# The sequence transform's four groups in one block, and E columns ahead of the tables' copies

## The chip, the cores and the metric

The kernel runs on one core of one Trainium2 chip. The metric is the device time of one execution in microseconds. A core has five engines with queues of their own: TensorE (PE, with weight loads shown as PEld), VectorE (DVE), ScalarE (ACT), GpSimd (POOL) and SyncE (SP), which here issues nearly all DMA transfers. Each engine works through its queue in order and waits for the others by semaphores. In this kernel the order is fixed by hand: the program text's order is the order in every queue.

## The reference

```python
X = np.fft.fft(x, axis=1)          # x: 8 batches, 3008 positions, 256 features
X = np.fft.fft(X, axis=2)
x = X.real.reshape(8 * 3008, 256)
gate = 1.0 / (1.0 + np.exp(-(x @ w_gate)))      # w_gate, w_val: 256 x 1536
val = x @ w_val
out = gate * val @ w_out                        # w_out: 1536 x 256
```

All is float32. The kernel uses the symmetries of the real transform: for a batch it computes three tables over positions k, pk (cosine part), qk (sine part) and ek (the contribution of feature 128, called E here), each of 1505 columns, and gets the hidden values of positions k and S - k from sums and differences of products of these.

## The kernel before

The main loop has 576 steps. A batch has 72 steps, in 6 chunks of 256 positions (the last has 225), and a chunk has 12 steps, one for each 128 hidden features. A step multiplies with pk and qk (front), forms the hidden product of the step before (gate), and adds to the output of two pairs of steps before (back):

```python
def front(p, fh):
    ...
    for g in range(2):
        mm(pa[:, g], G1[:, g, fs], pk[:, ks], g == 0, True)
    for g in range(2):
        mm(pb[:, g], G2[:, g, fs], qk[:, ks], g == 0, True)
    for g in range(2):                          # VectorE
        nc.vector.scalar_tensor_tensor(out=ae[:, g], in0=ek[:, ks], scalar=ge[:, g, f : f + 1],
                                       in1=pa[:, g], op0=ALU.mult, op1=ALU.add)
    nc.vector.tensor_tensor(z[:, :, 0], ae, pb, op=ALU.add)
    nc.vector.tensor_tensor(z[:, :, 1, ::-1], ae, pb, op=ALU.subtract)

def gate(p, fh, z):
    nc.vector.tensor_tensor(h[:, fh], z[:, 0], z[:, 1], op=ALU.mult)
    # ... then one or three sums sf of h on GpSimd

def back(p, part):
    for m in ORDER[part]:                       # 3 or 4 matmuls of h and sf into PO
        mm(PO[t][:, j, 0:n], wf[:, i, m - 1], move[m], ...)
```

A matmul of float32 stands in the trace as two records. The tiles pa, pb, ev, od and pe share four PSUM banks, which are given out in turn (psx, bufs=4). A bank is free when what reads it has read it.

Beside these steps, one batch ahead, the next batch's pk and qk are made. Its input x is first copied within DRAM into a mirrored form (mirror_x: xr), loaded (load_x: x4, one buffer), folded on GpSimd in 24 operations (fold_ops), and then transformed in four groups, one for each parity of k (blk) and each of cosine and sine (what). A group is 12 matmul pairs, the two of a pair on the two halves of the rows:

```python
    def both():
        for r in range(2 - blk):
            for q in range(N3 if blk == 0 else NQ):
                for par, sum_ in enumerate((ev, od)):
                    ...
                    mm(sum_[:, ks], w(wq)[rows], ST[0][rows, int(sn), q, c0 : c0 + n][:, ks], ...)

    def then():
        a = evp.tile([P, NE], F32, name="a", tag="a")[:, 0:n]
        nc.scalar.copy(a, ev)
        return lambda: places(d, blk, sn, a, od)       # two sums on VectorE into pk or qk

def whole(b, blk, what):
    _, then, both = seq_group(b, blk, what)
    both()
    return then()
```

The E tables of batches 1 to 7 are made together, once: e_load(b) loads feature 128 of a batch (single values of 4 bytes), e_fold adds on GpSimd, e_sums multiplies on TensorE and writes the result to DRAM, from where a batch's ek is loaded later. The tables of the transform (stab) are copied within DRAM into mirrored form too (mirror_tables: tr), and loaded again in that form (table_again), which all groups of batches 1 to 7 read.

Work of this kind is put at the end of numbered steps:

```python
def at(i, *fs):                # do fs at the end of step i
    side.setdefault(i, []).extend(fs)

def split(i, f, *args):        # f at step i, what it returns at step i + 1
    at(i, lambda: at(i + 1, f(*args)))
```

Of the kernel before, what the change touches and what calls it, by code (L numbers as in the profile page):

```python
# [51 lines left out]
def kernel(  # L52
# [57 lines left out]
    def load_x(b):  # L110
        X[b] = xp.tile([P, 4, NQ, D], F32, name="x4", tag="x4")
        for h in range(0, 4, 2):
            if b:
                nc.sync.dma_start(out=X[b][:, h : h + 2], in_=XR[b][:, h : h + 2])
            else:
                nc.sync.dma_start(out=X[b][0:NP, h : h + 2], in_=xf[b, :, h : h + 2])

    def mirrored(dst, src, full):


        copy = nc.sync.dma_start
        h, n = dst.shape[1], dst.shape[3] - full
        ops = [lambda: copy(out=dst[HP - 2 : HP, :, NQ - 1, full:],  # L123
                            in_=zero[:, :, 0:n].to_broadcast([2, h, n]))]

        def rows(par):
            copy(out=dst[par * HP : (par + 1) * HP, :, 0:N3], in_=src[0:HP, :, par:NQ:2])  # L127

        def mirror(par, q):
            t = M // 2 - 2 * q - par  # L130
            lo, p0, n = par * HP, t // NQ, HP - 2 * ((par, q) == (0, N3 - 1))
            copy(out=dst[lo : lo + n, :, N3 + q, full:].rearrange("p h d -> h p d"),  # L132
                 in_=src[p0 - n + 1 : p0 + 1, :, t % NQ, full:].rearrange("p h d -> h p d")[:, ::-1])
        for par in range(2):
            ops.append(lambda par=par: rows(par))
            ops += [lambda par=par, q=q: mirror(par, q) for q in range(N3)]
        return ops
# [3 lines left out]
    def mirror_x(b):  # L141
        XR[b] = dram.tile([P, 4, NQ, D], F32, name=f"xr{b}")
        return mirrored(XR[b], xf[b], 0)
# [17 lines left out]
    def mirror_tables():  # L161
        return mirrored(tr, stab, NE)
# [213 lines left out]
# [5 lines that stand above are left out]
    def seq_start(b):  # L381
        PQE[b] = (pqp.tile([P, NK], F32, name="pk", tag="pk"),
                  pqp.tile([P, NK], F32, name="qk", tag="qk"),
                  pqp.tile([P, NK], F32, name="ek", tag="ek"))
        if b:
            nc.sync.dma_start(out=PQE[b][2], in_=ed[b - 1 : b, :].to_broadcast([P, NK]))

    def seq_group(b, blk, what, other=None):
        return half(lambda q: W[b, blk][what][:, q, :], PQE[b][what], blk, what == 1, other)


    def e_load(b):
        nc.sync.dma_start(out=x8[:, b - 1], in_=xf[b, :, :, :, HD : HD + 1])  # L393
# [216 lines left out]
    def at(i, *fs):  # L610
        side.setdefault(i, []).extend(fs)

    def split(i, f, *args):

        at(i, lambda: at(i + 1, f(*args)))
# [11 lines left out]
        at(2 * c + (-3, -2, 1)[w], lambda j=j: weight_use(j))  # L627


    i0 = 2 * NPR  # L630
    quiet = lambda lo: (i for i in range(lo, 2 * len(pairs)) if not 3 <= i % i0 <= 7)
    calm = lambda lo: (i for i in range(lo, 2 * len(pairs)) if 3 <= i % i0 <= 7)
# [2 lines left out]
    at(i0 + 2, lambda: load_x(1))  # L635
    for b in range(1, B):
        at(i0 + 2 + b, lambda b=b: e_load(b))
    for i, f in zip(range(i0 + 3, 2 * i0), mirror_tables()):
        at(i, f)
    at(2 * i0 + 3, e_fold)  # L640
    split(2 * i0 + 5, e_sums)
    at(2 * i0 + 8, table_again)

    for b in range(B - 1):
        s0 = b * per
        if b:
            at(s0 - 5, lambda b=b: load_x(b + 1))

        def folds(f0=s0 - 1 if b else i0 + 8, b=b):
            for i, f in zip(quiet(f0), fold_ops(b + 1, 2)):  # L650
                at(i, f)
        at(s0 - 2 if b else i0 + 7, folds)
        groups = [s0 + i0 * k + 3 for k in (2, 3, 4, 5)] if b else [
            i0 * k + d for k in (4, 5) for d in (3, 6)]
        at(groups[0] - 2, lambda b=b: seq_start(b + 1))
        for j, g in enumerate(groups):
            split(g, whole, b + 1, 1 - j // 2, j % 2)
        if b < B - 2:
            for i, f in zip(calm(s0 + 2 * i0 + 9), mirror_x(b + 2)):
                at(i, f)  # L660

    fresh = None
# [72 lines left out]
```

## Time and profile before

| | |
|---|---|
| time, median of 3 | 2010.83 us (2010.72 to 2019.48) |
| span of the profiled execution | 2008.0 us |
| instructions | 28130 |
| granted TensorE clock, mean | 0.995 |
| DMA | 100.32 MB, mean 50 GB/s |

In the profile's rows an engine, an operation and its tiles are named as out<-in, and L100 is the helper that all matmuls go through, so matmuls are told apart by tiles. Busy time of an engine is not the same as use: a matmul's start-to-start distance shows what it costs in a stream, and is shorter than its duration, as matmuls are pipelined. SPq is SyncE's queue of DMA issues.

### The profile page before, as it was taken

The page shows a single profiled execution, that of the slowest core. Times are in us where ns is not written, and L with a number is a line of the kernel's source. Part 1 is how long each engine was busy: PE and PEld are TensorE (multiplying, and loading weights), DVE is VectorE, ACT ScalarE, POOL GpSimd, SP SyncE. Part 2 cuts the span into 40 slices and gives each one's busy share as a digit, 9 for nine tenths or more (in the row PEclk, how much of TensorE's full clock was granted, in tenths as well). Part 3 has the DMA queues.
Part 4 walks back from the last instruction along what each step waited for, and adds up shares of the span by engine and source line. Part 5 has one row for each costly group of instructions (what it writes and reads, how often), then busy time and mean ns, then how long its engine had stood idle before and what let it go on. Part 6 is the DMA issues. An engine that isn't in the chain of part 4 may idle for free.

```text
span 2008.0 us, 28130 instructions
## 1 busy us (share of the span) xinstructions
PE 1975.4 (98%) x9504; PEld 1738.0 (87%) x9504; DVE 1767.0 (88%) x3221; ACT 498.3 (25%) x876; POOL 1332.2 (66%) x1704
## 2 busy tenths in 40 slices
PE   6998999999999999999999999999999999999998
PEld 4887889888998889888898888988889888998888
DVE  7997988988899888998889888898889997898887
ACT  3422222222222222222222222222222222222221
POOL 3676867775578655777567765677657775555655
PEclk9998999999999999999999999999999999999999
DMA  7355202111200112001120011201211010000001
GB/s 270 93 142 139 81 11 75 23 51 46 74 20 27 43 43 83 12 27 43 48 79 10 27 48 48 74 10 32 69 41 55 15 32 11 11 16 16 11 16 26
DMA packets 160814, 100.32 MB, mean 50 GB/s; under 512 B 128419, under 2 KB 151715, under 8 KB 157994
## 3 DMA queue, kind: packets, MB, share of 16 engines
q1 hardware_dynamic: 158850, 98.00, 16.9%
q8 instruction: 76, 1.25, 0.3%
q10 hardware_dynamic: 1822, 0.54, 0.1%
q14 instruction: 66, 0.54, 0.1%
HBM read 73.74 MB, written 50.17 MB: 62 GB/s over the span
## 4 chain that ended last, share of the span: by engine, by line
PE 92%; DMA 3%; SPq 3%; DVE 1%; issue 0%; ACT 0%; POOL 0%; ACTq 0%; DVEq 0%; POOLq 0%
PE po L100 41%; PE pa L100 23%; PE pb L100 23%; PE ev L100 4%; SPq L132 1%; DMA ge<-G 1%; DMA st<-in_stab_dram 1%; SPq L127 1%; DMA xr<-in_xf_dram 1%; SPq L123 0%; PE ps L100 0%; DMA x<-in_xf_dram 0%; PE od L100 0%; SPq L393 0%; DMA raw<-in_moe_w_gate_dram 0%
## 5 line engine op out<-in xcount | busy, mean ns | idle before, releaser
L672 ACT ACTIVATE z<-z 128x512 f32<-128x512 f32 (+1 forms) x576 | 358.5, 622 | 1308.2 <-DVE z L451 1308.2
L447 DVE SCALAR_TENSOR_TENSOR ae<-ek,ge,pa 128x256 f32<-128x256 f32 (+1 forms) x1152 | 488.4, 464 | 159.4 <-PE pa L100 155.1
L100 PE MATMUL pa<-pk,G 128*128 128x256 f32 (+1 forms) x2304 | 585.4, 377 | 0.0
L100 PE MATMUL pb<-qk,G 128*128 128x256 f32 (+1 forms) x2304 | 582.1, 375 | 2.5 <-DVE ae L447 2.5
L100 PE MATMUL po<-sf,wf 128*128 128x256 f32 (+1 forms) x2304 | 534.7, 375 | 0.0
L466 POOL TENSOR_TENSOR sf<-h 128x256 f32<-128x256 f32 (+1 forms) x288 | 206.9, 718 | 443.4 <-DVE h L462 443.4
L100 PEld LDWEIGHTS pa<-pk,G 128*128 128x128 f32 x2304 | 436.8, 191 | 59.6 <-issue 11.9
L100 PEld LDWEIGHTS pb<-qk,G 128*128 128x128 f32 x2304 | 438.3, 190 | 52.7 <-DVE ae L447 4.1
L100 PEld LDWEIGHTS po<-sf,wf 128*128 128x128 f32 x2304 | 438.7, 191 | 48.8 <-POOL sf L468 0.3
L462 DVE TENSOR_TENSOR h<-z 128x512 f32<-128x512 f32 (+1 forms) x576 | 471.4, 818 | 0.0
L450 DVE TENSOR_TENSOR z<-ae,pb 128x512 f32<-128x512 f32 (+1 forms) x576 | 390.0, 677 | 61.3 <-DVE ae L447 1.8
L100 PE MATMUL po<-h,wf 128*128 128x256 f32 (+1 forms) x1728 | 412.7, 375 | 0.0
L451 DVE TENSOR_TENSOR z<-ae,pb 128x512 f32<-128x512 f32 (+1 forms) x576 | 386.4, 671 | 0.0
L100 PEld LDWEIGHTS po<-h,wf 128*128 128x128 f32 x1728 | 329.0, 190 | 36.4
L464 POOL TENSOR_TENSOR sf<-h 128x256 f32<-128x256 f32 (+1 forms) x288 | 206.4, 717 | 128.8 <-DVE h L462 118.5
L468 POOL TENSOR_TENSOR sf<-h,sf 128x256 f32<-128x256 f32 (+1 forms) x288 | 213.5, 741 | 22.6
L467 POOL TENSOR_TENSOR sf<-sf,h 128x256 f32<-128x256 f32 (+1 forms) x288 | 207.2, 719 | 22.6
L100 PE MATMUL ev<-st,x 63*128 63x376 f32 (+4 forms) x372 | 103.2, 420 | 6.7 <-DVE x L290 5.4
L100 PE MATMUL od<-st,x 63*128 63x376 f32 (+4 forms) x372 | 102.5, 418 | 0.0
L100 PEld LDWEIGHTS ev<-st,x 63*128 63x128 f32 (+1 forms) x372 | 65.1, 188 | 38.6 <-DVE x L290 5.8
L549 ACT COPY c<-po 128x512 f32<-128x512 f32 (+1 forms) x141 | 76.3, 579 | 47.7 <-PE po L100 47.1
L509 DVE STREAM_TRANSPOSE os<-c 128x256 f32<-128x256 f32 x192 | 83.8, 436 | 0.2
(91 smaller groups left out, 808.9 us busy)
## 6 DMA issues: line engine op xcount, KB each, us to landing
x<-xr SPq DMA_DIRECT2D x14, 1536.0 KB
out_dram<-os SPq DMA_DIRECT2D x288, 64.0 KB
xr<-in_xf_dram SPq DMA_DIRECT2D x14, 768.0 KB
xr<-in_xf_dram SPq DMA_DIRECT2D x35, 256.0 KB
ek<-ed SPq DMA_DIRECT2D x7, 752.5 KB
out_dram<-os SPq DMA_DIRECT2D x92, 56.0 KB
x<-in_xf_dram SPq DMA_DIRECT2D x2, 1512.0 KB
tr<-in_stab_dram SPq DMA_DIRECT2D x2, 1129.5 KB
```

Source lines behind the costliest of these rows:

```text
L100: nc.tensor.matmul(o, l, r, start=start, stop=stop, skip_group_check=True)
L447: nc.vector.scalar_tensor_tensor(out=ae[:, g], in0=ek[:, ks], scalar=ge[:, g, f : f + 1], in1=pa[:, g], op0=ALU.mult, op1=ALU.add)
L450: nc.vector.tensor_tensor(z[:, :, 0], ae, pb, op=ALU.add)
L451: nc.vector.tensor_tensor(z[:, :, 1, ::-1], ae, pb, op=ALU.subtract)
L462: nc.vector.tensor_tensor(h[:, fh], z[:, 0], z[:, 1], op=ALU.mult)
L464: tt(s[:, 2], h[:, 0, 0], h[:, 0, 1], op=ALU.subtract)
L466: tt(s[:, 0], h[:, 0, 1], h[:, 1, 1], op=ALU.add)
L467: tt(s[:, 1], s[:, 0], h[:, 0, 0], op=ALU.subtract)
L468: tt(s[:, 3], h[:, 1, 0], s[:, 1], op=ALU.subtract)
L509: nc.vector.transpose(os_[:, s, 0:nb, h, :], t[:, slot, 0 : nb * TB])
L549: nc.scalar.copy(t[:, 2 * j : 2 * j + 2, 0:n], PO[j][:, :, 0:n])
L672: nc.scalar.activation(z[:, 0], z[:, 0], AF.Sigmoid)
```

## The change

Four things move; no operation is added, removed or altered.

- The four groups of a batch stand one after another at the end of one step (3 i0 + 3 steps into the batch before; for batch 1 at step 5 i0 + 3), where they stood in four steps, in four chunks (for batch 1 in two). The sums on VectorE that follow a group come right after it, not a step later. The purpose is to change between the two kinds of matmul once in a batch.
- The copies of the tables start after the E columns are loaded (step 2 i0 - 2, before at i0 + 3, interleaved with them); the fold of E comes 9 steps later, its sums 10 steps later, and the reload of the tables 9 steps later.
- The load of x for a batch follows the block directly (before: 5 steps ahead of the next batch).
- The folds start 16 steps ahead of the batch in whose time they ran (for batch 2, 4 steps; for batch 1 as before), and the mirrored copies of x come earlier in the batch.

In the diff i0 is 12 steps, one chunk, per is 72, and quiet and calm are the steps of a chunk outside and inside positions 3 to 7.

```diff
-    for i, f in zip(range(i0 + 3, 2 * i0), mirror_tables()):
-        at(i, f)
-    at(2 * i0 + 3, e_fold)
-    split(2 * i0 + 5, e_sums)
-    at(2 * i0 + 8, table_again)
+    for i, f in enumerate(mirror_tables()):
+        at(2 * i0 - 2 + i, f)
+    at(3 * i0, e_fold)
+    split(3 * i0 + 3, e_sums)
+    at(3 * i0 + 5, table_again)
 
     for b in range(B - 1):
         s0 = b * per
-        if b:
-            at(s0 - 5, lambda b=b: load_x(b + 1))
-
-        def folds(f0=s0 - 1 if b else i0 + 8, b=b):
+        g0 = s0 + 3 * i0 + 3 if b else 5 * i0 + 3
+
+        def folds(f0, b=b):
             for i, f in zip(quiet(f0), fold_ops(b + 1, 2)):
                 at(i, f)
-        at(s0 - 2 if b else i0 + 7, folds)
-        groups = [s0 + i0 * k + 3 for k in (2, 3, 4, 5)] if b else [
-            i0 * k + d for k in (4, 5) for d in (3, 6)]
-        at(groups[0] - 2, lambda b=b: seq_start(b + 1))
-        for j, g in enumerate(groups):
-            split(g, whole, b + 1, 1 - j // 2, j % 2)
+        f0 = s0 - 4 * i0 // 3 if b > 1 else 5 * i0 + 8 if b else i0 + 8
+        at(f0 - 1, lambda f0=f0, folds=folds: folds(f0))
+        at(g0 - 2, lambda b=b: seq_start(b + 1))
+        for blk in (1, 0):
+            at(g0, *[lambda b=b, blk=blk, what=what: whole(b + 1, blk, what)() for what in range(2)])
         if b < B - 2:
-            for i, f in zip(calm(s0 + 2 * i0 + 9), mirror_x(b + 2)):
+            at(g0 + 1, lambda b=b: load_x(b + 2))
+            for i, f in zip(calm(s0 if b else 3 * i0), mirror_x(b + 2)):
                 at(i, f)
```

## The prediction

> **What bounds the kernel now.** I read the busy shares first, then the chain that ended last, the waits, and timelines of the places that they point to.
>
> ```profile
> PE 1975.4 (98%) x9504; PEld 1738.0 (87%) x9504; DVE 1767.0 (88%) x3221; ACT 498.3 (25%) x876; POOL 1332.2 (66%) x1704
> ```
>
> TensorE is busy 98% of the span, and 92% of the chain that ended last is PE. So only two kinds of time can be won: gaps between matmuls, and matmuls that start later than they could although PE never shows as idle. VectorE has 12% of slack, which is where a new bound could come from.
>
> The chain in order of time has one long break after the start-up, with these two waits beside it:
>
> ```profile
> 158.14 7.11 DMA x<-in_xf_dram
> 166.31 4.17 PE pe L100 x24
> ```
>
> ```profile
> POOL x L397 <- DMA x<-in_xf_dram: 6.8, 1, 6.8
> PE pe L100 <- POOL x L399: 6.8, 1, 6.8
> ```
>
> The joint E sums (tile pe) wait for GpSimd's e_fold, which waits for the last E column. Why that column is late stands in the timeline of SyncE's queue (start, length, line):
>
> ```profile
> 138.88 0.84 SPq L393 DMA_DIRECT2D x<-in_xf_dram  x1
> 139.78 5.66 SPq L132 DMA_DIRECT2D tr<-in_stab_dram  x1
> 145.48 0.84 SPq L393 DMA_DIRECT2D x<-in_xf_dram  x1
> 146.37 5.38 SPq L132 DMA_DIRECT2D tr<-in_stab_dram  x1
> 151.80 0.84 SPq L393 DMA_DIRECT2D x<-in_xf_dram  x1
> 152.68 5.42 SPq L127 DMA_DIRECT2D tr<-in_stab_dram  x1
> 158.14 0.83 SPq L393 DMA_DIRECT2D x<-in_xf_dram  x1
> ```
>
> A column costs the queue 0.84 us, and between any two columns stands a table copy of over 5 us. The windows view shows what PE's wait brings along (the columns are the stretch, its length, the busy time of PE, PEld, DVE, ACT and POOL, the granted TensorE clock, the DMA share and GB/s):
>
> ```profile
> 161.50:171.70 10.20, 5.39 (x27) 2.46 (x28) 0.39 (x1) 1.44 (x3) 5.20 (x10) 0.50 0.57 95
> ```
>
> For the second kind of time I read PE's timeline around one group of the sequence transform (a group is 24 matmul records, in 12 pairs of ev and od that run side by side on the two halves of the rows):
>
> ```profile
> 490.73 1.89 PE L100 MATMUL po<-sf,wf 128*128 128x256 f32 x8
> 492.55 0.43 PE L100 MATMUL ev<-st,x 63*128 63x189 f32 x1
> ...
> 492.82 0.32 PE L100 MATMUL ev<-st,x 63*128 63x189 f32 x1
> ...
> 494.50 0.33 PE L100 MATMUL ev<-st,x 63*128 63x188 f32 x1
> ...
> 494.76 1.13 PE L100 MATMUL pa<-pk,G 128*128 128x256 f32 x4
> 495.73 1.03 PE L100 MATMUL pb<-qk,G 128*128 128x256 f32 x4
> ```
>
> Elsewhere four pa records take 0.86 us from start to start of the next name, 0.216 us each. Eight po from 490.73 would let the next start at 492.46; ev starts at 492.55: 0.09 us lost. The first pair takes 0.27 us to the second, later pairs 0.16 to 0.17: 0.10 lost. After the last pair (494.50) pa could start at 494.66 and starts at 494.76: 0.10. The first four pa take 0.97 instead of 0.86: 0.11. So one group costs 0.40 us of changing over, and the profile shows none of it as idle.
>
> **What the Trainium skill says.** "TensorE: Matmul & The Clock Gate", What's actually happening: the array runs at half clock by default and at full clock only while recent windows of about 3.4 us were busy. This trace agrees: a wait of 6.8 us, and 0.50 of the clock for 10.2 us. The same page, The mechanism (row and column packing): weights load beside running matmuls only if they go to another row group, and packed tiles start about 4 ns apart. Pairs here start within 0.02 us of each other, and the loss on going from 128 rows to 63 and back is what the first half would give; that cause is my reading. "SBUF — State Buffer", SBUF: two separate sides: VectorE operations with two SBUF inputs and GpSimd operations hold a shared port exclusively, and the loser blocks. The trace agrees, one product h began just after a fold operation and took 1.78 us instead of 0.69:
>
> ```profile
> 347.92 1.27 POOL L280 TENSOR_TENSOR x<-x 128x510 f32<-128x510 f32 x1
> 347.96 1.78 DVE L462 TENSOR_TENSOR h<-z 128x512 f32<-128x512 f32 x1
> ```
>
> **The change, part by part.** No instruction is added or removed; all is order.
>
> (1) Groups in a block. Before, each of 7 batches has 4 groups apart: 28 changes over. After, 4 follow one another: 7. Saved 21 x 0.40 = 8.4 us. Against it stand the seams inside a block. A group takes two of the four PSUM banks, so the third needs the banks of the first, and the fourth those of the second. Freeing them takes one copy on ScalarE (0.47 us, line 365) and two sums on VectorE (0.54 us each, lines 370 and 373), some 1.7 us with the hand-overs. The third group follows the second, of 12 wide pairs at 0.31 us (3.7 us): hidden. The fourth follows the third, of 12 narrow pairs at 0.16 (2.0 us): just hidden, or 0.1 to 0.3 us late. I take 0.2 x 7 = 1.4 us. Left: 7.0 us.
>
> (2) E sums. PE's step with them begins with pa at 155.86, the next pa at 170.42: 14.56 us, where such a step takes 3.45. The four pa at 170.42 then take 1.77 instead of 1.03, 0.74 more at the half clock. Together 11.85 us lost. After, the seven columns are issued one behind another from about 121 us (where the first stands now) with 0.84 us each; even with waits in the queue they are out by 140 and, at 7.1 us of landing, in by about 150. The fold comes 9 steps later and the sums 10, so nothing is needed before 178 us. Margin nearly 30 us. What stays is the sums: 24 records in 4.17 us at half the clock, so 2.1 at the full one, and a change over of 0.4 to 0.5: 2.6 us. Saved 11.85 - 2.6 = 9.2 us.
>
> (3) The table copies begin 7 steps later and their reload 9 steps later, the first group of batch 1 moves by 12 steps. The reload has 22 steps of 3.24 us (71 us) to land, before it had 19. Neutral. The x loads start right after a block; the first has only 4 to 5 steps (13 to 16 us) to its fold. In the trace such a load was issued at 302.06 and had moved its data by 312. Neutral.
>
> (4) GpSimd's folds start 16 steps ahead of a batch (b over 1) instead of 1. Same work, but 7 of the 24 steps now lie in the short last chunk (225 columns, 2.85 us a step on PE), and no group stands inside the run of folds, where before one came at step 27 and let VectorE catch up. The delay from the last pa to its ae, read in the timelines, is 0.42 us when VectorE keeps up. In a run of folds it rose by 1.7 to 1.9 us in four steps, fell by 1.3 in the eight after them, and peaked at 2.8 before the group. Carrying these slopes on, with nearly no slack in the short chunk, I get peaks of 3.7 to 4.3 us. PE stops where the banks of a step aren't free two steps later: a delay of about 3.7 us in the short chunk, 4.2 in a full one. So it touches: I take 0.25 us in each of 6 batches, 1.5 us.
>
> Sum: 8.4 - 1.4 + 9.2 - 1.5 = 14.7 us saved; 2010.8 - 14.7 = 1996.1, said as 1996 us.
>
> **Rivals.** First, VectorE becomes the bound in the folds: each fold operation can hold it by 1.1 us (1.78 less 0.69), and if the delay passes the limit by 1.5 to 2 us in every batch, 6 to 7 batches give back 10 to 14 us: about 2007. For it: no group breaks the run any more and the short chunk has no slack. Against it: in the first batch the delay stood at 3.5 us in steps of full length, without a gap in PE. Second, the wait of the E sums was useful: in it VectorE's delay fell from 2.5 to 0.4 us. Without it the arrears stay until the first block, and E's own sums on VectorE add over 3. If that stops PE, some 3 us of the 9.2 return: 1999. Against it: the E sums themselves pause PE for 2.6 us first. Third, the seams of a block cost as much as a change over, because banks come free late: then part 1 brings nothing, about 2003. Fourth, all hidden losses vanish and neither seams nor VectorE cost anything: 2010.8 - 17.6 = 1993.
>
> **Range and chances.** The two savings are read off one trace to within 1 us. What can vary is how much VectorE and the seams return, 0 to 14 us; 17.6 us, 0.9%, is all that there is to save by this reading. So low 1990 (some other slack falls out as well), high 2005. The 2% lines are at 1971 and 2051: nothing here can reach them. Faster by over 2% 0.01, within 2% 0.97, slower 0.02.
>
> **What would show it.** Step 1: 7 blocks of 96 ev and od records in PE's timeline, with one entry and one exit, no start later than 0.3 us inside. Step 2: no POOL wait on the E load, pe at about 190 us in about 2 us, no clock of 0.50 after the start. Step 4: waits of pa or pb on VectorE of a few us in all, at the end of the short chunk and the start of the next batch. I am wrong if those waits exceed 5 us, if the fourth group of each block waits, or if the sums still wait for columns.

## The result and the profile after

| | before | changed |
|---|---|---|
| median, us | 2010.83 | 1992.56 (1992.14 to 1993.95, 4 runs) |
| ratio to before | | 0.990, interval 0.9873 to 0.9926 |
| profiled span, us | 2008.0 | 1992.2 |
| first pa of step 20 to first pa of step 575, us | 1864.90 | 1847.00 |

The last row is worked out from the starts in PE's timeline. It is needed because the start-up before step 20 varies by itself: step 20 began at 126.94 us in the profile before, at 129.03 in the changed one, and between 127.41 and 136.18 in the experiments below. From step 20 on the times repeat to 0.01 us, as the changed kernel run again (e10) shows. There the change is worth 17.90 us, and that is the number to explain.

The busy shares of the changed kernel's page say little: PE was and is nearly full (98% before, 99% now), and VectorE went from 88% to 89%.

What answers to the lines of before is in three timelines of the changed kernel. First, SyncE's queue issues all seven E columns in one go, with no table copy in between:

```profile
123.43 20.41 SPq L393 DMA_DIRECT2D x<-in_xf_dram  x7
```

Second, the fold of E on GpSimd and the E sums on TensorE:

```profile
189.21 0.72 POOL L397 TENSOR_TENSOR x<-x 126x42 f32<-126x42 f32 x1
...
190.32 1.03 PE L100 MATMUL pa<-pk,G 128*128 128x256 f32 x4
...
192.05 1.89 PE L100 MATMUL po<-sf,wf 128*128 128x256 f32 x8
193.87 2.09 PE L100 MATMUL pe<-st,x 126*7 126x377 f32 x24
...
195.89 1.13 PE L100 MATMUL pa<-pk,G 128*128 128x256 f32 x4
```

No idle time stands in brackets behind the fold or the sums, and the 24 records take 2.09 us, half of the 4.17 before, as the clock stays full (1.00 in the windows view of 189 to 200 us). From pa to pa the step takes 5.57 us instead of 14.56.

Third, PE around the block of batch 2: entry, the seam between the third and the fourth group, exit. (A group is six pairs of matmuls and so 12 pairs of records; a pair below is a pair of records.)

```profile
434.75 1.89 PE L100 MATMUL po<-sf,wf 128*128 128x256 f32 x8
436.57 0.58 PE L100 MATMUL ev<-st,x 63*128 63x376 f32 x1
...
436.99 0.48 PE L100 MATMUL ev<-st,x 63*128 63x376 f32 x1
...
446.10 0.33 PE L100 MATMUL ev<-st,x 63*128 63x188 f32 x1
...
446.27 0.33 PE L100 MATMUL ev<-st,x 63*128 63x189 f32 x1
...
448.12 0.32 PE L100 MATMUL ev<-st,x 63*128 63x188 f32 x1
...
448.41 1.13 PE L100 MATMUL pa<-pk,G 128*128 128x256 f32 x4
```

The entry still loses 0.09 us (eight po from 434.75 end their turn at 436.48), the first pair still takes 0.42 to the second where later wide pairs take 0.31 to 0.32, and the exit is as it was. But this now happens once in a batch, and at the seam the pairs keep their step of 0.17 us: 446.10, 446.27, and 11 steps later 448.12. VectorE's timeline shows why the fourth group finds its banks free:

```profile
445.42 0.54 DVE L373 TENSOR_TENSOR qk<-od,a 128x376 f32<-128x376 f32 x1
```

This last reader of the second group's banks ends at 445.96, 0.31 us before the fourth group starts. The other six blocks have the same steps.

PE's own rows show none of the changing over as idle time. The row of the weight loads does, contrary to what the prediction says of the whole profile: at every return to the main stream the load for pa has idle time before it for which the profile names no releaser ("issue"). These are the waits of before, then of the changed kernel:

```profile
PEld pa L100 <- issue: 11.9, 29, 1.3
PEld pa L100 <- issue: 2.3, 8, 0.6
```

28 groups and the E sums are 29 returns; seven blocks and the E sums are eight. The idle time here is that of PEld and is not the loss itself, but the count is the number of changes over.

### The profile page after: what moved, and what is told of

The parts are those of the page before. It is cut to its first block, busy times and chain, and to the rows that moved or that the text cites. A ratio compares the mean times of both kernels' runs of the same rounds, so it can differ in the third digit from the quotient of the medians.

```text
span 1992.2 us, 28166 instructions
## 1 busy us (share of the span) xinstructions
PE 1965.1 (99%) x9504; PEld 1737.3 (87%) x9504; DVE 1777.8 (89%) x3221; ACT 497.2 (25%) x876; POOL 1348.3 (68%) x1704
## 4 chain that ended last, share of the span: by engine, by line
PE 96%; DMA 2%; DVE 1%; ACT 0%; issue 0%; POOL 0%; SPq 0%; ACTq 0%; DVEq 0%; POOLq 0%
PE po L100 43%; PE pa L100 24%; PE pb L100 24%; PE ev L100 4%; DMA ge<-G 1%; DMA st<-in_stab_dram 1%; PE od L100 1%; PE ps L100 0%; DMA raw<-in_moe_w_val_dram 0%; DVE ae L447 0%; POOL wx L236 0%; PE pe L100 0%; DVE z L451 0%; DVE wx L232 0%; DVE os L509 0%
## 5 line engine op out<-in xcount | busy, mean ns | idle before, releaser
L462 DVE TENSOR_TENSOR h<-z 128x512 f32<-128x512 f32 (+1 forms) x576 | 480.6, 834 | 0.0
L468 POOL TENSOR_TENSOR sf<-h,sf 128x256 f32<-128x256 f32 (+1 forms) x288 | 207.8, 721 | 22.6
L100 PE MATMUL ev<-st,x 63*128 63x376 f32 (+4 forms) x372 | 98.5, 417 | 7.9 <-DVE x L290 5.9
L100 PE MATMUL od<-st,x 63*128 63x376 f32 (+4 forms) x372 | 97.4, 413 | 0.0
```

Source lines behind the costliest of these rows:

```text
L100: nc.tensor.matmul(o, l, r, start=start, stop=stop, skip_group_check=True)
L468: tt(s[:, 3], h[:, 1, 0], s[:, 1], op=ALU.subtract)
```

## Experiments

The column "steady" is the time from step 20's first pa to step 575's, read as in the table above; it has none of the start-up's variation. It comes from the one execution of each kernel that has a trace, so it is one reading each. Ratios are to the kernel before, with their intervals.

| run | median, us | ratio | steady, us | steady, less the changed kernel |
|---|---|---|---|---|
| e10, changed again | 1994.02 | 0.9902 (0.9888 to 0.9916) | 1847.00 | 0 |
| e1, block only | 2005.02 | 0.9955 (0.9943 to 0.9967) | 1857.18 | 10.18 |
| e2, groups apart | 2003.76 | 0.9953 (0.994 to 0.9966) | 1855.27 | 8.27 |
| e9, two and two | 1996.98 | 0.9919 (0.9905 to 0.9933) | 1849.79 | 2.79 |
| e3, columns first | 1996.06 | 0.9912 (0.9899 to 0.9926) | 1847.68 | 0.68 |
| e4, sums late | 1994.23 | 0.9905 (0.9891 to 0.9919) | 1847.00 | 0 |
| e6, folds back | 1996.57 | 0.9925 (0.9908 to 0.9942) | 1847.00 | 0 |
| e8, filler | 2007.49 | 0.9973 (0.9966 to 0.998) | 1859.76 | 12.76 |
| e5, dense folds | 2038.73 | 1.0127 (1.0112 to 1.0142) | 1889.08 | 42.08 |
| e7, full rows (computes something else) | 2071.85 | one execution | 1925.17 | 78.17 |

### The two parts apart

e1, the block with the old E part:

```diff
-    for i, f in enumerate(mirror_tables()):
-        at(2 * i0 - 2 + i, f)
-    at(3 * i0, e_fold)
-    split(3 * i0 + 3, e_sums)
-    at(3 * i0 + 5, table_again)
+    for i, f in zip(range(i0 + 3, 2 * i0), mirror_tables()):
+        at(i, f)
+    at(2 * i0 + 3, e_fold)
+    split(2 * i0 + 5, e_sums)
+    at(2 * i0 + 8, table_again)
```

> The block as in the changed kernel; the E columns, the tables' copies, the E sums and the reload as in the kernel before. Theory (two separate losses, a change over of 0.385 us for each group and one E wait): only the groups' part is won, 2010.8 - 8.1 = 2002.7 us, and the E wait of some 7 us and the half clock are back. Rival (the wait of E is useful, as VectorE catches up in it): nearer to the changed kernel, 1995 to 1999.

The waits of e1 show the E wait back, 0.6 us longer than in the kernel before (PE waits the same 7.4 us for GpSimd):

```profile
POOL x L397 <- DMA x<-in_xf_dram: 7.4, 1, 7.4
```

Steady, e1 is 1864.90 - 1857.18 = 7.7 us better than before and 10.2 worse than the changed kernel. With the 0.6 us of longer wait added back, the block is worth 8.3. The median stands 2.3 us above the expected 2002.7, but the kernel before, run beside it, had a median of 2012.84, and against that e1 is 7.8 us faster. The useful wait would have brought e1 below 2002.7, to 1995 to 1999: the rival is out.

e2, the changed kernel with the groups in four steps:

```diff
-        for blk in (1, 0):
-            at(g0, *[lambda b=b, blk=blk, what=what: whole(b + 1, blk, what)() for what in range(2)])
+        for j in range(4):
+            split(g0 + 2 * j, whole, b + 1, 1 - j // 2, j % 2)
...
-            at(g0 + 1, lambda b=b: load_x(b + 2))
+            at(g0 + 7, lambda b=b: load_x(b + 2))
```

(and 5 * i0 + 11 in place of 5 * i0 + 8 for the folds of batch 2)

> The changed kernel, but the four groups in four steps, two steps apart (at g0, g0+2, g0+4, g0+6), the load of x six steps later and the fold of batch 2 three steps later; all else as changed. Theory: 21 changes over more at 0.385 us, 1992.6 + 8.1 = 2000.7 us. Rival (the gain comes from where the groups and folds stand, not from the number of changes over): 1992.6 to 1995.

PE's timeline of e2 has the change over at both ends of every group:

```profile
437.47 1.89 PE L100 MATMUL po<-sf,wf 128*128 128x256 f32 x8
439.29 0.58 PE L100 MATMUL ev<-st,x 63*128 63x376 f32 x1
...
443.29 1.13 PE L100 MATMUL pa<-pk,G 128*128 128x256 f32 x4
```

Steady it is 8.27 us above the changed kernel: 21 changes over more, 0.394 us each. With the 9.63 us of the E sums, read from the timelines further down, that makes up the whole 17.90, so nothing is left for where groups and folds stand.

e9, the block cut in two:

```diff
-            at(g0, *[lambda b=b, blk=blk, what=what: whole(b + 1, blk, what)() for what in range(2)])
+            at(g0 + 2 * (1 - blk), *[lambda b=b, blk=blk, what=what: whole(b + 1, blk, what)() for what in range(2)])
```

(with the load of x two steps and the folds of batch 2 one step later)

> The changed kernel with the block cut in two: the two wide groups at g0, the two narrow ones two steps later. Theory (each change over costs 0.385 us, one more in each of 7 batches): 2.7 us above the changed kernel, and in the trace 7 more entries and exits. Rival (a block of four is what counts, or the places of groups): as e2, 8 us above, or as changed.

2.79 us for 7 changes over, 0.399 each. The cost goes with their number: 7, 14, 28 of them give 0, 2.79, 8.27.

### What the change over is

e7 lets each matmul of the groups use all rows:

```diff
-                        rows = slice(par * HP, par * HP + HP - 1 - (par and q % N3 == N3 - 1))
+                        rows = slice(0, P)
```

It leaves out the split by parity, and the two of a pair run one after the other.

> The changed kernel with every matmul of the groups of batches 1 to 7 on all 128 rows, where the two of a pair take one half of the rows each. It leaves out the split by parity, so the output is not the reference's; the two of a pair can no longer run side by side, which makes it slower by about 7 x 12 = 84 us. What counts is the change over at the block's entry and exit. Theory (the loss comes from going from full rows to half rows and back, as weights of overlapping rows can't be loaded ahead): with full rows throughout the next start is in step, entry within 0.02 us of the stream, no longer first pair, no loss in the first pa. Rival (any change of tile, width or bank costs it): 0.4 us as before.

PE's timeline of e7 at a block's entry and exit:

```profile
445.64 1.89 PE L100 MATMUL po<-sf,wf 128*128 128x256 f32 x8
447.37 0.80 PE L100 MATMUL ev<-st,x 128*128 128x376 f32 x2
...
470.24 0.49 PE L100 MATMUL od<-st,x 128*128 128x188 f32 x2
470.57 1.02 PE L100 MATMUL pa<-pk,G 128*128 128x256 f32 x4
471.43 1.03 PE L100 MATMUL pb<-qk,G 128*128 128x256 f32 x4
```

Eight po from 445.64 end their turn at 447.37, and ev starts at 447.37. The first two ev take 0.63 us (od follows at 448.00), as later ones do; the last two od take 0.33 to the pa, in step; and the four pa at the exit take 0.86. All four pieces of the loss are gone, though tile, width and banks change as before.

The weight loads show it too. In the changed kernel the load for a block's first ev starts together with its matmul; in e7 it starts 0.22 us ahead of it, beside the last po. The two loads, changed kernel first:

```profile
436.57 0.18 PEld L100 LDWEIGHTS ev<-st,x 63*128 63x128 f32 x1 [0.33 <-DVE z L451]
447.15 0.41 PEld L100 LDWEIGHTS ev<-st,x 128*128 128x128 f32 x2
```

(The z in brackets is not the cause: the block of batch 1, at 272.96, has the same 0.33 us with no releaser named.) Of the eight waits of pa's load in the changed kernel, e7 has one left:

```profile
PEld pa L100 <- issue: 0.6, 1, 0.6
```

That one belongs to the E sums, which e7 leaves as they are, and they correct the reading of the cause. They use 126 of the 128 rows, and 7 columns of the array each, with four such matmuls side by side (their records start 7 ns apart). In the changed kernel, eight po from 192.05 end their turn at 193.78 and pe starts at 193.87: 0.09 us lost. From the last pe to pa it is 0.41 us, where from four pe to the next four it is 0.30: 0.11 lost. The first four pa take 0.96 instead of 0.86: 0.10. So some 0.3 us are lost around matmuls whose rows are not halved; only the loss in the first pair (0.10) is seen with half rows alone.

Nor are overlapping rows the obstacle. In the main stream, and in the line at 447.15, the load for a matmul of 128 rows runs beside another matmul of 128 rows. The prediction cites the Trainium skill, "TensorE: Matmul & The Clock Gate", The mechanism, for loads that run beside matmuls only into another row group. The same section also names a background weight buffer as a place for them, and by this trace the row groups alone do not decide.

What fits all of this: the loss comes with going between matmuls that take the whole array and matmuls that share it side by side, by rows or by columns, and at such a change the next load does not run ahead. e7 takes away the halving and the sharing at once, so it can't tell them apart; the E sums speak for the sharing. Why the load does not run ahead, no run shows.

### Order of the columns, or later sums

e3 keeps the columns first, with fold and sums at their old steps:

```diff
-    at(3 * i0, e_fold)
-    split(3 * i0 + 3, e_sums)
+    at(2 * i0 + 3, e_fold)
+    split(2 * i0 + 5, e_sums)
```

> The changed kernel with the E fold and the E sums at their old steps (27 and 29), the columns still ahead of the tables' copies. Theory A (the order of the transfers is what counts): the seven columns are out by 144 us and in by about 150, the fold at about 152 and the sums at about 160 do not wait, time as changed, 1992.6 within 1. Theory B (the later sums are what counts): the sums wait again for several us and the clock falls, 1997 to 2002.

e4 keeps the late fold and sums, with the columns between the copies as before:

```diff
-    for i, f in enumerate(mirror_tables()):
-        at(2 * i0 - 2 + i, f)
+    for i, f in zip(range(i0 + 3, 2 * i0), mirror_tables()):
+        at(i, f)
```

> The changed kernel with the columns and the tables' copies interleaved as before, but the E fold and sums at the later steps (36 and 39). Theory A (order counts): a wait is left, 1997 to 2002. Theory B (later sums count): the columns are in by 166 us, the fold comes at 180, no wait, 1992.6 within 1. If both e3 and e4 are at 1992.6, either half would have done.

In e3's timeline the sums come 32 us earlier than in the changed kernel and hardly wait:

```profile
159.93 0.71 POOL L397 TENSOR_TENSOR x<-x 126x42 f32<-126x42 f32 x1
...
161.28 2.31 PE L100 MATMUL pe<-st,x 126*7 126x377 f32 x24 [0.39 <-POOL x L399]
```

The fold no longer waits for a column; the 0.39 us come from GpSimd reaching it late. With the sums taking 2.31 instead of 2.09 us, that is most of the 0.68 us. In e4 nothing waits. So either half alone brings nearly all of the 9.6 us of the E part, and the later sums alone all of it; the two are two cures of one wait.

### VectorE's delay

e6 starts the folds where they started before:

```diff
-        f0 = s0 - 4 * i0 // 3 if b > 1 else 5 * i0 + 8 if b else i0 + 8
+        f0 = s0 - 1 if b else i0 + 8
```

> The changed kernel with the folds starting one step ahead of the batch, as before, not 16 steps ahead; they end two steps before the block. Theory (the start of the folds costs and brings nothing as long as VectorE's delay stays below the limit): 1992.6 within 0.5. Rival 1 (the earlier start is part of the gain, as a block at the end of the folds would wait for GpSimd): PE waits 1 to 3 us at the blocks, 1999 to 2013. Rival 2 (the predicted cost of folds in the short chunk is real but hidden in another gain): faster than changed by 1 to 2 us.

Steady it equals the changed kernel to 0.01 us. Its median, 4 us above the expected 1992.6, is not explained by that: the execution with the trace took 1994.50 us, and the others, up to 1999.89, left none. In the part that the trace shows, the earlier folds cost and bring nothing.

How near the limit the changed kernel comes is seen in step 5 of batch 3, where VectorE's delay is at its peak in the folds. From its timeline, the step's four pa and the two ae that read them:

```profile
803.92 1.03 PE L100 MATMUL pa<-pk,G 128*128 128x256 f32 x4
...
808.19 0.86 DVE L447 SCALAR_TENSOR_TENSOR ae<-ek,ge,pa 128x256 f32<-128x256 f32 x2
```

The last of the pa starts at 803.92 + 3 x 0.216 = 804.57, so the delay is 3.62 us, where 0.42 is usual. PE keeps its step all the same. Just after the E sums it is higher still, 4.03 in step 41, without a gap.

e8 adds idle writes on VectorE at that place, one more per step from batch to batch:

```diff
+        if b > 1:
+            for i in range(s0, s0 + 6):
+                at(i, *[lambda: nc.vector.memset(fill, 0.0)] * (b - 1))
```

> The changed kernel with idle writes (192 columns of zeros to a tile that nobody reads) added on VectorE in the first six steps of batches 2 to 6, 1 in each step of batch 2, 2 in batch 3, up to 5 in batch 6, just where VectorE's delay behind PE peaks (3.6 us). It measures the limit that the prediction put at 4.2 us. Theory (limit as worked out from the four PSUM banks, or from h, which the output matmuls need three steps later): the delay goes to about 4.2 to 5 and no higher, and PE waits grow from batch to batch, none or under 1 us in batch 2, several in batch 6. Rival (GpSimd's sums are what PE waits for, as with dense folds): PE waits for sf, at a delay below 4.

Two of the writes, and the end of VectorE's work on step 2 of batch 3, from VectorE's timeline of e8; then PE in step 4, which takes the same banks again:

```profile
806.36 0.54 DVE L660 MEMSET fill<- 128x192 f32 x2
...
808.27 0.68 DVE L452 TENSOR_TENSOR z<-ae,pb 128x512 f32<-128x512 f32 x1
```

```profile
808.05 1.03 PE L100 MATMUL pa<-pk,G 128*128 128x256 f32 x4
809.10 1.10 PE L100 MATMUL pb<-qk,G 128*128 128x256 f32 x4
```

What PE waited for in the stretch of batch 6:

```profile
PE pb L100 <- DVE z L452: 1.9, 6, 0.4
```

A write takes 0.218 us, but two take 0.54: from start to start a further write costs 0.325, and the first one some 0.21. By these distances, the six steps carry an estimated 1.3, 3.2, 5.2, 7.1 and 9.1 us more on VectorE in batches 2 to 6. From one block's start to the next the changed kernel takes 240.48 us; e8 takes 240.48, 241.98, 242.94, 244.18 and 245.62, so it loses 0, 1.50, 2.46, 3.70 and 5.14 us. The first 1.3 us are free; of what comes on top, PE pays two thirds or somewhat more.

The limit shows at the first pb that is late. In step 2 of batch 3 the delay is 4.23. Two steps later pb starts 1.05 us after pa, where 0.86 is usual, because z, which reads step 2's pb, ends only at 808.95; pb follows 0.15 us behind. No idle time stands in brackets. In batches 4 to 6 the first late pb comes after delays of 4.58, 4.14 and 4.46 and is late by 0.53, 0.10 and 0.42. Delay less lateness is 4.0 each time. So PE waits for the PSUM banks, read by VectorE, and the limit is 4.0 us in these steps, where two steps last 6.11 us. Where they last 6.47, as in step 5 of the changed kernel, there is more room: pb of step 7 starts 0.82 us after z has ended, 0.67 more than the 0.15, so with a delay of 3.62 the limit is 4.3. In step 41, after the E sums, 0.27 us of room are left, and 4.03 and 0.27 make 4.3 again.

In batches 2 and 6 the losses are as expected, 0 and 5.14 us. In the stretch of batch 6 no wait of PE for sf or h stands, so the rival is out and h is not the limit. The delay was expected to stay at 5 and below; it rose to 5.52, 6.15, 6.48 and 6.80 in batches 3 to 6.

e5 puts the 24 fold operations into 24 steps in a row:

```diff
-            for i, f in zip(quiet(f0), fold_ops(b + 1, 2)):
+            for i, f in zip(range(f0, 2 * len(pairs)), fold_ops(b + 1, 2)):
```

> The changed kernel with one fold operation in each of 24 steps in a row, also in the steps in which GpSimd makes the output's sums. Theory (VectorE's delay behind PE has a limit near 4 us, and the fold's pauses keep it below): the delay passes the limit, and PE waits 1 to 3 us in each of 7 batches, 2000 to 2013 us. Rival (VectorE has slack enough however the folds lie): 1992.6 within 1.

It is far slower than expected, and not for the expected reason. Its waits:

```profile
PEld po L100 <- POOL sf L467: 27.9, 24, 2.0
PE po L100 <- POOL sf L467: 19.5, 17, 1.6
```

PE waits for GpSimd's sums sf. VectorE's delay in the folds stays at 4.1 us and less, but for 4.63 in step 41, after the E sums, where pb comes 0.33 us late; that is all that VectorE's limit takes of the 42 us. From 230.0 and from 1305.2 us on, the granted clock is also 0.50 for 3.4 us. In these steps GpSimd has the step's own sums (0.72 us each), the output's sums and a fold operation (1.27 us for the one shown before); in the 30 us from 785 it is busy for 28.80, and its queue runs over first. The theory of e5 fell; the pauses of the folds protect GpSimd.

## Why the prediction was right, point by point

**Time.** 1992.56 us lies in the range. The saving was put at 14.7 us and is 18.3 by the medians, 17.9 without the start-up. The sum's two gains were right, its two losses did not come. The steady saving of 17.9 is near the 17.6 that the two gains make alone.

**(1) Changes over.** Predicted 21 x 0.40 = 8.4 us, measured 8.27 (e2), each 0.394 to 0.399 (e2, e9). The count and the cost of one, read off the trace, were right and needed no cause. The reading of the cause was too narrow: half rows are not needed, as the E sums lose 0.3 us with 126 rows, and overlapping rows do not keep a load from running ahead in the main stream. That the profile shows none of the loss as idle time held for PE, not for the weight loads.

**(1) Seams.** Predicted 1.4 us of loss, measured none. The term that was too large is the wait of the fourth group: I had 1.7 us of clearing against 2.0 us of matmuls and took 0.2 us of delay from it; the trace has 0.31 us to spare.

**(2) E sums.** Predicted 9.2 us. From the two timelines: 11.85 lost before, 5.57 - 3.45 = 2.12 in the step and 0.10 in its first pa after, so 9.63. The sums take 2.09 us, as the halved 4.17 said; the change over is some 0.3 us, where 0.4 to 0.5 was taken. The columns did not go out at 0.84 us each: together they held the queue for 20.41 us, and were out by 143.8 against 140 predicted. The margin of nearly 30 us covered that, and the fold does not wait. 8.27 + 9.63 = 17.90, the whole steady difference.

**(3) Reload and loads of x.** Neutral, as predicted; nothing in the steady sum is left for them.

**(4) VectorE in the folds.** Predicted 1.5 us, measured 0 (e6 equals the changed kernel). What was too large is the peak of the delay: the slopes carried on gave 3.7 to 4.3 us; it peaks at 2.5 in the short chunk and at 3.6 after it. The limit was about right. It was put at 4.2 in a full chunk, and e8 and the room in the changed kernel give 4.0 to 4.3; it was put at 3.7 in the short chunk, and there a delay of 2.49 leaves 1.34 us from z to pb, 1.19 more than the 0.15, so 3.7. That the delay touches the limit was wrong; that it comes near, to 0.67 us in a step of the folds and 0.27 after the E sums, was right.

**Rivals.** The first (VectorE becomes the bound) and third (seams) did not come. The second half came: after the E sums the delay did rise to 4.0, but it stays under the 4.3 of that step. The fourth, 1993 us, is what happened.

## What to carry to other kernels

On an engine that shows as 98% busy, compare start-to-start distances with the steady step, and read the weight loads' row: changes between matmuls on the whole array and matmuls that share it cost 0.3 to 0.4 us each here and stand in no wait of PE; putting such matmuls together saved each change that it took away. Before spending on the order of transfers, ask whether the reader can simply come later; here ten steps of delay alone cured the wait. Where two engines feed a third, measure the delay and its limit with a known filler, as the first engine to run over may be another than the one watched.

## What was not expected of the hardware

- Going between the whole array and half rows: 0.09 us at the entry, 0.10 in the first pair, 0.20 at the exit; with the whole array throughout, none (e7). Going to the E sums' 126 rows and 7 columns and back: 0.09 and 0.21.
- At such a change the next weight load starts with its matmul, and the wait stands in PEld's row alone: 29 times before, 8 in the changed kernel, once in e7.
- A delay of VectorE behind PE of up to 4.0 to 4.3 us was free with four PSUM banks (e8).
- From step 20 on, the changed kernel, its repeat and two kernels of other order (e4, e6) agree to 0.01 us in 1847, while step 20 began at 127.41 to 133.76 us in these four profiles.
- Seven transfers of 11.8 KB in values of 4 bytes held SyncE's queue for 20.41 us when issued together (the second 8.57 us, the five after it about 2 each), where one between other transfers took 0.84. Why is not tested.
